# Reordering the pair loop of a chunk-selecting attention with a routed MoE behind it

## The chip, the cores and the metric

One core of one Trainium2 chip runs the whole program. The metric is the device time of one execution in microseconds; lower is better. The engines have these names in the profile: PE is TensorE (matmuls and transposes; PEld its weight loads), DVE is VectorE, ACT is ScalarE, POOL is GpSimd, and SP is the engine that issues most of the plain DMAs.

## The reference

```python
ub = np.sum(np.maximum(q * k_min, q * k_max), axis=-1)      # 24 chunks of 32 keys, per query
ub = np.where(causal, ub, -1e9)
top_chunks = np.argsort(ub, axis=-1)[..., -6:]
scores = scale * np.matmul(q, k.transpose(0, 1, 3, 2))
mask = sel & (pos[:, None] >= pos[None, :])                 # sel: the key's chunk is in top_chunks
scores = np.where(mask, scores, -1e9)
attn = softmax(scores)
x = (attn @ v), heads side by side                          # 3072 tokens of 512
expert_idx = np.argmax(x @ w_gate, axis=1)                  # top 1 of 8 experts
out[mask] = gate_w * (np.maximum(x[mask] @ w1[e], 0) @ w2[e])
```

There are 4 batches of 8 heads, 768 positions, head dimension 64. The expert layer has 512 inputs and 1024 hidden units. All inputs and outputs are float32.

## The kernel before

The attention works on pairs of heads of one batch: 16 pairs (`NP`), pair `i` being heads 2·hp and 2·hp+1 of batch b, with `b, hp = divmod(i, 4)`. The 128 partitions hold the two heads side by side. The loop over `i` is a schedule written out by hand: under `tc.manual_schedule` every engine executes its instructions in the order in which they stand in the program. Each pass mixes work of several pairs. For pair `i` it has the scores, the exponentials and the products with v; for `n = i + 1` the chunk selection; for `m = i + 2` the transposes of k and q; for pairs `i - 1` and `i - 2` the sums for the softmax, the gate's logits and the rows of x that go to the experts.

The steps, with the names that the prediction uses:

- `k_mm(hf)` transposes three 128-row tiles of k into a PSUM tile `pk`; `k_a` (ACT, L203) writes them as bf16 into KTE; `k_v` (DVE, L197 and L198) reduces them to each chunk's maximum and minimum; `kse` (DVE, L208 to L210) makes from these the operand KSD of the bounds.
- `q_mm(hf)` transposes q into `pq`; `q_v` (DVE, L223) copies it to `qT`; `q_a` takes the absolute value on ACT (`qA`, L228) and writes head 1's part of QSB (L231), and puts head 0's part (a POOL copy, L229) into the list `late`, which `flush(late)` issues.
- `ub` (L238) is four products of KSD with `qT` and four with `qA`: the upper bounds, chunk by query, in `pu`. `ub_a` (ACT, L245) copies them, `sel_mm` (L250) transposes them into `pt`, and `sel_v` (DVE) adds the causal bias `cbias` (L256), finds the eight largest of each row twelve times (L264) and marks in `nsel` what falls outside the six best (L267).
- `mask` (L274) transposes `nsel` into `pm`, and `mask_a` (ACT, L280) copies it into extra rows of QSB, so that the score product itself adds the mask.
- `scores(i, u)` (L298) makes one of seven units of scores (`units`: query block 0 has units 0 and 1, block 1 units 2 to 6; each 768 columns over two heads). `exps` is the ACT exponential (L314), with POOL's `affine_select` (L318) on diagonal tiles. `av(i, u)` (L331) is the product with v, added up in `po`; `add` (DVE, L339) adds up the exponentials for the row sums; `o_ev(i, qb)` copies `po` out (L344 on ACT, L346 on DVE).
- `ud` (L362 and L374, four column tiles of the array) makes the row sums and the gate's products of pair i-1; `ud_a` (L380), `lgp_mm` (L385), `lgp_v` (L391, L395), `x_mm` (`px`, L415) and `x_v` (L420) turn them into logits and rows. The logits are added on POOL by `sums` (L403, L406), which `flush(sums_)` issues.
- In the pairs with hp = 1 of batches 1 to 3 (called router pairs) also the routing of the batch before: `logits`, `rank_mm` (a PSUM tile `pr`, L467), `expo`, `rank_v`, `gates`. Its scatter of rows to DRAM (POOL, L493) is spread over that pair and the next by `spread`.

PSUM is shared out in three pools: `ps_m` has three buffers under one tag and holds `pk`, `pq`, `pu`, `pt`, `pm`, `pl` and `px` in turn; `ps_s` has two, for score units and `pr`; `ps_o` has one, for `po`.

PE's products come in three array shapes: the full array (scores except unit 6, and all float32 transposes), two column tiles of 64 (`av`, `ub`, the `nsel` transposes and score unit 6) and four column tiles of 32 (`ud`).

The weights of the experts come in 32 pieces by POOL's DMA queue (`load_w`, L157), spread over the pairs by `npiece`. `load` fetches k, q and v by SP's. `first_pair` builds constants and takes pair 0 up to its fourth score unit, in an order of its own. After the last pairs an expert table is computed on DVE (`table`), rows are gathered by POOL (`gather`, L593), transposed by DMA (`x_in`, L605), and each of 25 row tiles goes through `up` (L641) and `down` (L653), then out by a scatter (L661).

Of the kernel before, what the change touches and what calls it, by code (L numbers as in the profile page):

```python
# [24 lines left out]
def kernel(  # L25
# [33 lines left out]
    c0s = (0, 128, 192)  # L59
    NU = 7  # L60
# [23 lines left out]
    pm64 = const.tile([128, 1], FP32)  # L84

# [17 lines left out]
    def consts_first():  # L103
# [17 lines left out]
        nc.gpsimd.memset(cbias[:], 0.0)  # L121
        for t in range(3):
            nc.gpsimd.affine_select(out=cbias[:, t], in_=cbias[:, t], pattern=[[320, 2], [-CH, NCH]],
                                    compare_op=ALU.is_ge, fill=NEG, base=128 + c0s[t], channel_multiplier=1)
        nc.gpsimd.memset(nsel[:], 0.0)
# [10 lines left out]
        return colf  # L136
# [7 lines left out]
    def consts_last():  # L144
        nc.gpsimd.memset(dcol[:], 0.0)
        nc.gpsimd.memset(dcol[:, DC:DC + 1], 1.0)
        nc.gpsimd.memset(wgb[:], 0.0)

# [33 lines left out]
    def prep_steps(i):  # L182
# [70 lines left out]
        def sel_v():  # L253
            pt = s["pt"]
            ubm = work.tile([128, 3, 2, 2, NCH], FP32, tag="ubm")
# [85 lines left out]
    def o_ev(i, qb, act=False):  # L341
        ot = work.tile([128, 384], FP32, tag="ot", bufs=3, name="ot")
        if act:
            nc.scalar.activation(ot[:], st[i][f"po{qb}"][:], AF.Copy)  # L344
        else:
            nc.vector.tensor_copy(out=ot[:], in_=st[i][f"po{qb}"][:])  # L346
        st[i][f"ot{qb}"] = ot
# [326 lines left out]
    npiece = [1, 2, 2, 2, 2, 1, 1, 2, 2, 1, 1, 2, 2, 2, 4, 1]  # L674
    assert sum(npiece) == 4 * E - 4
# [6 lines left out]

    def first_pair():
# [4 lines left out]
        colf = consts_first()  # L688
# [34 lines left out]

        kt(0)
        for hf in range(2):
            nc.vector.tensor_copy(out=qsb[0:64, 1, ts(hf, 384)], in_=pq[64:128, hf, 0:384])
            nc.gpsimd.tensor_copy(out=qsb[0:64, 0, ts(hf, 384)], in_=s["qT"][0:64, hf])
        consts_last()
        consts_route(colf)
        prep[0]["ub"]()  # L730
        prep[0]["ub_a"]()
        kt(1)
        spin(8)
        prep[0]["sel_mm"]()
        spin(20)
        ubm = work.tile([128, 3, 2, 2, NCH], FP32, tag="ubm")
        top8 = work.tile([128, 3, 2, 2, 8], FP32, tag="top8")
        pm = ps_m.tile([64, S], BF16, tag="m")
        for _ in range(2):
            load_w(next(wnext))  # L740

        def select(hf):
            nc.vector.tensor_tensor(ubm[:, :, hf], s["pt"][:, :, hf, :, 0:NCH],
                                    cbias[:, :, hf].unsqueeze(2).to_broadcast([128, 3, 2, NCH]), ALU.add)
            for t in range(3):
                for hd in range(2):
                    nc.vector.max(out=top8[:, t, hf, hd], in_=ubm[:, t, hf, hd])
            nc.vector.tensor_tensor(nsel[:, :, hf, :, 0:NCH], ubm[:, :, hf],
                                    top8[:, :, hf, :, TOPK - 1:TOPK].to_broadcast([128, 3, 2, NCH]), ALU.is_lt)

        def mask_mm(hf):
            for t in range(3):
                nc.tensor.transpose(pm[:, ds(128 + 320 * hf + c0s[t], 128)],
                                    nsel[:, t, hf].rearrange("p a n -> p (a n)"), ident_b[:])

        def mask_in(hf):
            cols = ds(128 + 320 * hf, 320)
            nc.scalar.activation(qsb[64:64 + NCH, 0, cols], pm[0:NCH, cols], AF.Copy)
            nc.vector.tensor_copy(out=qsb[64:64 + NCH, 1, cols], in_=pm[32:32 + NCH, cols])

        select(0)
        mask_mm(0)
        mask_in(0)
        spin(8)
        scores(0, 0)
        exps(0, 0)
        select(1)
        scores(0, 1)
        exps(0, 1)
        mask_mm(1)  # L770
        mask_in(1)
        for _ in range(2):
            load_w(next(wnext))
        p1 = prep[1]
        for hf in range(2):
            p1["k_mm"](hf)
            p1["k_v"](hf)
            p1["k_a"](hf)
        p1["kse"]()
# [3 lines left out]
        p1["q_mm"](0)  # L783
        scores(0, 3)
        p1["q_mm"](1)
        av(0, 1)
        for hf in range(2):
            p1["q_v"](hf)
            p1["q_a"](hf, 0)
        load(2, "q")  # L790
        wg_v = moe_w_gate.rearrange("(c p) e -> p c e", p=128)
        nc.sync.dma_start(out=wgb[0:64, :, 0:E], in_=wg_v[0:64])
        nc.sync.dma_start(out=wgb[64:128, :, E:2 * E], in_=wg_v[64:128])
        exps(0, 2)
        exps(0, 3)
        o_ev(0, 0)
# [3 lines left out]
        for hf in range(2):  # L800
            p1["q_a"](hf, 1)

# [4 lines left out]
    with tc.manual_schedule(engines={PE, POOL, SP, DVE, ACT}):  # L807
        first_pair()
        early_table = table(True)
        for i in range(NP):  # L810
# [9 lines left out]
            for g in range(4):  # L820
                if (i, g) == (0, 0):
                    pass
                elif g == 0:
                    if i < NP - 1 and not (hp == 2 and b > 0):
                        pieces(i, 2 if router else 1)
                    if router:
                        logits()
                    for u in (2, 3):
                        scores(i, u)
                        exps(i, u)  # L830
                    run(rout, i - 2, "x_mm", 1)

                    xv_first = i < NP - 1 and (hp != 2 or b == 0)
                    if xv_first:
                        run(rout, i - 2, "x_v", 1)
                    if i < NP - 1:
                        add(i - 1, 5)
                    add(i - 1, 6)
                    if not xv_first:
                        run(rout, i - 2, "x_v", 1)  # L840
                    av(i, 0)
                    av(i, 1)
                    dve_ot = not router and i < NP - 2
                    if dve_ot or i == NP - 1:
                        o_ev(i, 0, not dve_ot)
                    add(i, 1)
                    run(prep, n, "ub")
                    run(prep, n, "ub_a")
                    if not dve_ot and i < NP - 1:
                        o_ev(i, 0, True)  # L850
                    if i < NP - 1:
                        load(n, "v")
                elif g == 1:
                    for u in (4, 5):
                        scores(i, u)
                        exps(i, u)
                    run(prep, n, "sel_mm")
                    if i > 0:
                        run(prep, m, "k_mm", 0)
                        run(prep, m, "k_a", 0)  # L860
                    if router:
                        rank_mm()
                    run(prep, n, "sel_v")
                    if router:
                        expo()
                        rank_v()
                        gates()
                    if i > 0:
                        run(prep, m, "k_v", 0)
                    av(i, 2)  # L870
                    av(i, 3)
                    add(i, 3)
                    flush(late)
                    if i < NP - 1:
                        pieces(i, 4)
                    scores(i, 6, True)
                    exps(i, 6)
# [165 lines left out]
```

The softmax here doesn't subtract the row's maximum and nothing guards it: scores larger than these inputs give would overflow.

## Time and profile before

| | |
|---|---|
| time, median of 3 runs | 357.44 us (356.74 to 357.91) |
| profiled execution | 357.17 us, of which the profile's span is 355.5 us |
| mean granted TensorE clock | 0.988 |
| L362 of pair 1 / of pair 14 starts at | 38.79 us / 218.25 us |
| intervals between L362 groups, pairs 2 to 14 | 13.38, 13.40, 13.50, 14.15, 14.22, 13.83, 13.50, 14.16, 13.97, 14.29, 13.51, 14.15, 13.40 us |
| first score unit of pair 0, its unit 4, pair 1's unit 2 | 14.29, 22.22, 31.27 us |
| first expert product | 236.43 us |

The intervals show the pace of the loop: the group L362 is issued once a pair, always at the same place of the order. Pairs 5, 9 and 13 are the router pairs. In rows of the timeline the first number is the start in us, the second the time until the last of the group ends, and in brackets stands idle time before it and what ended that. In rows of busy time by stage the columns are the stretch, its length, and PE, PEld, DVE, ACT and POOL busy (with counts), then the granted clock, the DMA engines' share and GB/s. A row of waits gives who waited for whom, the total in us, how often, and the longest.

### The profile page before, as it was taken

What the parts mean: (1) busy time and instruction counts of PE and PEld (TensorE: products, weight loads), DVE (VectorE), ACT (ScalarE), POOL (GpSimd) and SP (SyncE); (2) the same over time, 40 slices, a digit from 0 to 9 for tenths busy, and PEclk for the clock granted to TensorE, in tenths of its full rate; (3) what the DMA queues carried; (4) which work ended last, traced back from release to release, by engine and by line L of the source; (5) the groups of instructions that cost most, each with busy time, mean ns of one, the idle gap of its engine ahead of it and who ended that gap; (6) DMA issues with size and microseconds to landing.
All of it is one profiled execution on the core that took longest, in us unless ns stands there. A gap on an engine that the chain in (4) does not pass through costs nothing. (4 is left out here: it accounts for less than half of the span.)

```text
span 355.5 us, 7585 instructions
## 1 busy us (share of the span) xinstructions
PE 329.2 (93%) x2382; PEld 177.2 (50%) x2392; DVE 229.5 (65%) x776; ACT 230.4 (65%) x373; POOL 186.7 (53%) x300
## 2 busy tenths in 40 slices
PE   7889999999999999999999999977995899999992
PEld 7545656556555555555565555534441344444440
DVE  6688999999999999999999999941730000000000
ACT  2588788788796887886887977613323454544551
POOL 8515434536475437284355477583574556655323
PEclk9999999999999999999999999989998999999999
DMA  9998998899585897765979954969694999998962
GB/s 175 205 209 152 167 184 169 153 190 167 104 211 113 161 178 155 152 171 114 186 137 181 182 122 113 209 124 197 137 227 121 227 185 216 194 231 160 216 154 80
DMA packets 132071, 59.83 MB, mean 168 GB/s; under 512 B 122811, under 2 KB 122813, under 8 KB 132032
## 3 DMA queue, kind: packets, MB, share of 16 engines
q1 hardware_dynamic: 120640, 29.91, 43.5%
q0 software_dynamic: 11392, 29.42, 40.0%
q8 instruction: 21, 0.34, 0.4%
q14 instruction: 18, 0.15, 0.1%
HBM read 56.14 MB, written 10.51 MB: 188 GB/s over the span
## 5 line engine op out<-in xcount | busy, mean ns | idle before, releaser
L339 DVE TENSOR_TENSOR Pa<-Pa,Pr 128x768 f32<-128x768 f32 (+2 forms) x109 | 80.5, 742 | 4.3
L318 POOL TENSOR_SCALAR_AFFINE_SELECT Pr<-Pr 128x256 f32<-128x256 f32 x78 | 36.9, 492 | 77.9 <-ACT Pr L314 77.9
L314 ACT ACTIVATE Pr<-ps 128x768 f32<-128x768 f32 x79 | 62.6, 819 | 10.7 <-ACT KTE L203 4.3
L653 PE MATMUL py<-w_all,hT 128*128 x220 | 52.4, 379 | 3.0 <-issue 1.7
L298 PE MATMUL ps<-QSB,KTE 128*128 128x384 bf16 (+4 forms) x352 | 50.4, 283 | 1.5 <-ACT Pr L314 0.2
L661 POOL DMA_INDIRECT out_dram<-y,ti_all x28 | 28.0, 1001 | 37.2 <-ACT y L660 32.1
L298 PEld LDWEIGHTS <-KTE 128*128 128x128 bf16 (+1 forms) x352 | 26.5, 102 | 28.4 <-issue 22.0
L641 PE MATMUL ph<-w_all,KTE 128*128 x116 | 31.1, 413 | 6.3 <-ACT h__3986 L644 3.6
L653 PEld LDWEIGHTS <-hT 128*128 128x128 bf16 x224 | 21.8, 98 | 29.5 <-issue 1.8
L314 ACT ACTIVATE Pa<-ps 128x768 f32<-128x768 f32 x32 | 26.0, 812 | 14.0 <-PE ps L298 12.6
L660 ACT ACTIVATE y<-py,gt_all 128x512 f32<-128x512 f32 x27 | 18.6, 687 | 25.0 <-PE py L653 19.4
L203 ACT ACTIVATE KTE<-pk 64x384 bf16<-64x384 f32 x60 | 29.3, 488 | 7.1 <-DVE kmn L198 6.7
L493 POOL DMA_INDIRECT xs_dram<-xrow,sli x24 | 25.6, 1065 | 7.8 <-issue 5.7
L641 PE MATMUL ph<-w_all,QSB 128*128 x94 | 22.6, 379 | 1.6 <-DMA QSB<-xgqT 1.5
L641 PEld LDWEIGHTS <-KTE 128*128 128x128 bf16 x120 | 12.3, 104 | 23.0 <-issue 9.6
L280 ACT ACTIVATE QSB<-pm 24x640 bf16<-24x640 bf16 x30 | 20.8, 692 | 2.8 <-PE pm L274 2.1
L614 DVE TENSOR_TENSOR ti_all<-xgqA,inv_i 128x1 int32<-128x1 int32 x9 | 1.4, 160 | 30.7 <-DMA xgqA<-xs_dram,grow 26.1
L157 POOL DMA_DIRECT2D w_all<-in_moe_w_dram x32 | 21.1, 663 | 0.0
L197 DVE TENSOR_REDUCE kmx<-pk 128x12 f32<-128x384 f32 x32 | 17.6, 549 | 3.2 <-PE pk L192 3.0
L593 POOL DMA_INDIRECT xgqT<-xs_dram,grow x14 | 14.8, 1058 | 9.1 <-issue 6.2
L593 POOL DMA_INDIRECT xgqA<-xs_dram,grow x14 | 14.4, 1029 | 8.6 <-issue 4.7
L614 DVE TENSOR_TENSOR ti_all<-xgqT,inv_i 128x1 int32<-128x1 int32 x8 | 1.3, 159 | 25.7 <-DMA xgqT<-xs_dram,grow 20.9
(318 smaller groups left out, 635.9 us busy)
## 6 DMA issues: line engine op xcount, KB each, us to landing
w_all<-in_moe_w_dram POOLq DMA_DIRECT2D x32, 512.0 KB
out_dram<-y,ti_all POOLq DMA_INDIRECT x28
t__115<-in_k_dram SPq DMA_DIRECT2D x2, 192.0 KB
t__118<-in_q_dram SPq DMA_DIRECT2D x2, 192.0 KB
t__121<-in_v_dram SPq DMA_DIRECT2D x2, 192.0 KB
t__218<-in_k_dram SPq DMA_DIRECT2D x2, 192.0 KB
t__240<-in_q_dram SPq DMA_DIRECT2D x2, 192.0 KB
t__243<-in_v_dram SPq DMA_DIRECT2D x2, 192.0 KB
```

Source lines behind the costliest of these rows:

```text
L157: nc.gpsimd.dma_start(out=dst, in_=src.rearrange("(c p) f -> p c f" if n < 2 else "(p c) f -> p c f", p=128))
L203: nc.scalar.activation(kte[0:64, hd, ts(hf, 384)], pt[64 * hd:64 * hd + 64, :], AF.Copy, bias=0.0, scale=0.125)
L280: nc.scalar.activation(qsb[64:64 + NCH, hd, 128:S], s["pm"][32 * hd:32 * hd + NCH, 128:S], AF.Copy)
L298: nc.tensor.matmul(ps[ds(h * n, n), hd, ds(c0, w)], lhsT=kte[:, hd, ds(kb * 128 + h * n, n)], rhs=qsb[:, hd, ds(qb * 384 + 384 - w, w)], s ...
L314: nc.scalar.activation(P[:], ps[:, :, 0:384], AF.Exp)
L318: nc.gpsimd.affine_select(out=pd, in_=pd, pattern=[[0, 2], [1, 128]], compare_op=ALU.is_ge, fill=0.0, base=0, channel_multiplier=-1)
L339: nc.vector.tensor_tensor(acc[:, :, 384 - w:384], acc[:, :, 384 - w:384], P[:, :, ds(c0, w)], ALU.add)
L493: d = nc.gpsimd.indirect_dma_start(out=xs_dram[:], out_offset=bass.IndirectOffsetOnAxis(ap=sli[:, u:u + 1], axis=0), in_=bst[b][f"xrow{u % ...
L593: d = nc.gpsimd.indirect_dma_start(out=xg_bufs[j % XB].bitcast(I32), out_offset=None, in_=xs_dram[:], in_offset=bass.IndirectOffsetOnAxis( ...
L641: nc.tensor.matmul(ph[:, fh, :], lhsT=xT[:, c, :], rhs=w_all[:, ds(wo + (c * F + fh * 512), 512)], start=(c == 0), stop=(c == NDC - 1), sk ...
L653: nc.tensor.matmul(py[:], lhsT=hT[:, c, :], rhs=w_all[:, ds(wo + (W1W + c * DM), DM)], start=(c == 0), stop=(c == NFC - 1))
L661: d = nc.gpsimd.indirect_dma_start(out=out[:], out_offset=bass.IndirectOffsetOnAxis(ap=fs[j]["ti"], axis=0), in_=y[:], in_offset=None, bou ...
```

## The change

It rewrites the order of the pair loop and of `first_pair`.

- In the loop, selection of the next pair (`sel_mm`, `sel_v`) moves up beside units 2 and 3; `mask` goes between the transposes of k and `av` 2; `ud` stands between `av` 2 and `av` 3; `mask_a` follows `ud_a` on ACT; `av` 4, 5 and 6 stand together at the end, followed by `ub` and `ub_a` of pair i+2. `k_a` stands ahead of `k_v` in both halves. `flush(sums_)` moves to the end of each pair, `add(i, 5)` to the same pair's end.
- `o_ev` is on ACT by default, except for block 0 of pair 0.
- A one-element POOL copy `pace` out of `ubm` stands ahead of `flush(late)`, so that POOL's q copies follow the first step of `sel_v`.
- In `first_pair` the bounds of pair 0 come directly with queries on the partitions (`bounds`: five blocks of 128 queries, two products of 48 columns each), without `ub`, `ub_a` and `sel_mm`; constants of their own (`cb0`, `ns0`) stand in for `cbias` and `nsel`, which are built later. `consts_late` (routing constants, gate weights) moves to the end of pair 0.
- The four weight pieces inside `first_pair` go; `npiece` now covers all 32.

The diff, cut to its core:

```diff
-    def o_ev(i, qb, act=False):
+    def o_ev(i, qb, act=True):
...
-    npiece = [1, 2, 2, 2, 2, 1, 1, 2, 2, 1, 1, 2, 2, 2, 4, 1]
-    assert sum(npiece) == 4 * E - 4
+    npiece = [2, 3, 2, 2, 2, 2, 1, 2, 2, 2, 1, 2, 3, 2, 3, 1]
+    assert sum(npiece) == 4 * E
...
+        def bounds(js):
+            pt = ps_m.tile([128, len(js), 2, NCH], FP32, tag="m", name="pt0")
+            for n, j in enumerate(js):
+                for w_, nm in ((0, "qT"), (1, "qA")):
+                    nc.tensor.matmul(pt[:, n], lhsT=s[nm][:].rearrange("p a c -> p (a c)")[:, ds(128 * j + 128, 128)],
+                                     rhs=KSD[0][:, w_, :, 0:NCH], start=(nm == "qT"), stop=(nm == "qA"),
+                                     skip_group_check=True)
+            pts_.append(pt)
...
+        qsb_in(0)
         kt(0)
...
         consts_last()
-        consts_route(colf)
-        prep[0]["ub"]()
-        prep[0]["ub_a"]()
+        consts_bias()
+        bounds(halves[0])
+        select(0)
+        qsb_in(1)
+        spin(4)
+        bounds(halves[1])
         kt(1)
-        spin(8)
-        prep[0]["sel_mm"]()
-        spin(20)
...
-        for _ in range(2):
-            load_w(next(wnext))
...
+        p1["k_mm"](0)
+        p1["k_a"](0)
+        mask_mm(1)
...
+        p1["k_v"](0)
+        p1["k_mm"](1)
         load(2, "k")
         av(0, 0)
         scores(0, 2)
-        p1["q_mm"](0)
+        exps(0, 2)
+        p1["k_a"](1)
+        p1["k_v"](1)
+        p1["kse"]()
         scores(0, 3)
...
         for hf in range(2):
+            p1["q_mm"](hf)
             p1["q_v"](hf)
             p1["q_a"](hf, 0)
         load(2, "q")
-        exps(0, 2)
+        av(0, 1)
         exps(0, 3)
-        o_ev(0, 0)
+        o_ev(0, 0, False)
...
+            if i > 0:
+                if i < NP - 1 and not (hp == 2 and b > 0):
+                    pieces(i, 2 if router else 1)
+                if router:
+                    logits()
+                for u in (2, 3):
+                    scores(i, u)
+                    exps(i, u)
+                run(rout, i - 2, "x_mm", 1)
+                run(prep, n, "sel_mm")
+                add(i - 1, 6)
...
+                run(prep, n, "sel_v")
+                if n < NP:
+                    nc.gpsimd.tensor_copy(out=pace[:], in_=st[n]["ubm"][:, 0, 0, 0, 0:1])
+                    flush(late)
...
+                av(i, 0)
+                av(i, 1)
+                o_ev(i, 0)
...
+            for u in (4, 5):
+                scores(i, u)
+                if u == 5:
...
+                        if router:
+                            rank_mm()
+                            expo()
+                            rank_v()
+                            gates()
+                        run(prep, m, "k_mm", 0)
+                        run(prep, m, "k_a", 0)
+                        run(prep, n, "mask")
+                exps(i, u)
+            if i > 0:
+                add(i, 1)
+                run(prep, m, "k_v", 0)
+            av(i, 2)
+            run(rout, i - 1, "ud")
+            run(rout, i - 1, "ud_a")
+            if i > 0:
+                run(prep, n, "mask_a")
+            av(i, 3)
+            add(i, 3)
...
+            scores(i, 6, True)
+            exps(i, 6)
...
+            run(rout, i - 1, "lgp_mm")
+            run(rout, i - 1, "x_mm", 0)
...
+            run(rout, i - 1, "lgp_v")
+            run(rout, i - 1, "x_v", 0)
+            run(prep, m, "k_mm", 1)
+            run(prep, m, "k_a", 1)
+            if n < NP:
+                for u in (0, 1):
+                    scores(n, u)
+                    exps(n, u)
+            run(prep, m, "k_v", 1)
+            for hf in range(2):
+                run(prep, m, "q_mm", hf)
+                run(prep, m, "q_v", hf)
+                run(prep, m, "q_a", hf, 0)
+            for hf in range(2):
+                run(prep, m, "q_a", hf, 1)
...
+            run(prep, m, "kse")
...
+            av(i, 4)
+            av(i, 5)
+            av(i, 6)
...
+            o_ev(i, 1)
+            run(prep, m, "ub")
+            run(prep, m, "ub_a")
+            flush(sums_)
```

## The prediction

> **What bounds the kernel now.** I read the engine line of the page first, then busy time by stage, then waits inside the pair loop, then the timeline of one pair. About 200 of the 355.5 us are the sixteen head pairs, and the edits are nearly all there.
>
> ```profile
> PE 329.2 (93%) x2382; PEld 177.2 (50%) x2392; DVE 229.5 (65%) x776; ACT 230.4 (65%) x373; POOL 186.7 (53%) x300
> ```
>
> ```profile
> 65.57:79.07 13.50, 13.43 (x116) 7.65 (x113) 12.61 (x38) 11.20 (x19) 6.42 (x13) 1.00 0.87 170
> ```
>
> The second row is one plain pair, from its group L362 to the next one's: 13.50 us with PE busy 13.43, DVE 12.61, ACT 11.20. The page's average hides that two engines are nearly full here. The waits from 40 to 225 us:
>
> ```profile
> PEld px L415 <- ACT KTE L203: 3.9, 13, 0.4
> ...
> ACT KTE L203 <- DVE kmn L198: 5.2, 13, 0.5
> ...
> DVE lgt L395 <- POOL lg L406: 2.4, 6, 0.4
> ```
>
> DVE waits for almost nothing else: it has about 13.1 us of work a pair and 0.4 us of wait for POOL's sums. PE's own waits are small and come once a pair. In the pair at 65.57 I find, by comparing equal groups, about 0.27 us at score unit 5, 0.1 at `px` and under 0.1 twice more. So PE's floor is near 13.05 us, and a full relief of DVE can give at most 0.45 us a pair.
>
> [...] readers of one PSUM tile take turns in program order, whichever is first.
>
> ```profile
> 9.49 1.03 DVE L726 CAST QSB<-pq 64x384 bf16<-64x384 f32 x2 [0.56 <-ACT qT L716]
> ...
> 71.55 0.98 ACT L203 ACTIVATE KTE<-pk 64x384 bf16<-64x384 f32 x2 [0.39 <-DVE kmn L198]
> 72.59 0.31 PEld L415 LDWEIGHTS px<-ident_f,ot 128*128 128x128 f32 x3 [0.28 <-ACT KTE L203]
> ```
>
> In line 1 DVE waits for ACT's read of `pq`, in line 2 ACT for DVE's read of `pk`. Line 3 shows a second rule: the three `ps_m` buffers go round, and `px` may start only when the tile three allocations earlier (`pk` of half 1) has been read. [...] Here a group of three transposes takes 0.38 us before another full-array group (76.50 to 76.88) and 0.47 before a two-tile group (72.59 to 73.06), so some 0.1 to 0.16 us a change. [...] L406 takes 1.54 us for two beside the adds, 0.39 us for one away from them.
>
> **The change, part by part.**
>
> *Groups.* Before, a pair goes: full; `av` 0, 1 and `ub`; full; `av` 2, 3, unit 6, the four-tile `ud`, `pm`, `av` 4, 5; full; `av` 6. That is three full and three two-tile stretches with one four-tile group inside: eight changes. After: full; `av` 0, 1; full; `pm`, `av` 2, `ud`, `av` 3, unit 6; full; `av` 4, 5, 6, `ub`. Eight again, so nothing is saved on PE and the floor stays 13.05.
>
> *Outputs on ScalarE.* Two DVE copies of 0.55 us (0.47 each from start to start) become ACT copies of 0.50. DVE falls to 12.2, ACT rises from 11.2 to about 12.2. DVE then isn't the limit, and no longer waits for POOL's sums, which move to the pair's end. What is late next is ACT, and what it orders.
>
> *A plain pair after*, with t = 0 at unit 2, from these rows: 0.33 a score unit or three transposes (0.38 the first of a kind), 0.65 an `av` (0.70 the first), 0.1 to 0.16 a mode change, 1.18 `ub` with its change, exp 0.70 from start to start, KTE or Q copies 0.49. Unit 2, 3, `px`, `pt` to 1.44; `av` 0, 1 to 2.95; unit 4, 5, `pk` to 4.07; `pm`, `av` 2 to 5.13; `ud` to 6.23, its second half starting at 5.79. ACT: the new output copy waits for `av` 1 (3.1 to 3.6; exp 4 is queued behind it, price nothing because ACT had idled), exp 4 to 4.3, KTE to 5.3, exp 5 to 6.0. Then the first chain:
>
> ```profile
> 79.74 0.51 PE L374 MATMUL pu<-ot,wgb 128*32 128x192 f32 x8
> ...
> 80.38 0.49 ACT L380 ACTIVATE ud<-pu 128x384 f32<-128x384 f32 x1 [0.34 <-PE pu L374]
> 80.89 1.41 ACT L280 ACTIVATE QSB<-pm 24x640 bf16<-24x640 bf16 x2
> ...
> 82.31 0.49 PE L415 MATMUL px<-ident_f,ot 128*128 128x128 f32 x3
> ```
>
> Copy of `ud` 0.64 after its half begins, then both mask copies, 2.6 us in all before the `pm` buffer is free: 5.79 + 2.61 = 8.40. Today two `av` fill that span. After, PE has only `av` 3, unit 6 and `pl` in it, and is at `px` (three allocations after `pm` now) at 7.79. **Stall one: 0.61 us.** Then `pk` half 1 ends at 9.28. The change puts KTE ahead of the reduces on it, [...] the second chain is KTE 0.98 (9.28 to 10.26), two reduces 0.93, q copies 0.93, `kse` 0.56: KSD is ready at 12.72. PE reaches `ub` at 12.50. **Stall two: 0.25 us.** Unit 2 of the next pair comes at 12.78 + 1.18 = 13.96, against 13.45 before. ACT's last copies end at 14.69, 0.73 into the next pair, before `pt` needs them at 1.02; DVE's `nsel` at 3.85 is in time for `pm` at 4.07.
>
> *Router pair*, 14.15 before. `pr` is now the second score buffer after unit 4, so it waits for exp 4, behind the output copy: about 0.8 us. The logits stand ahead of the selection on DVE and `pl` waits a little for the reduces; `px` comes at about 9.6 instead of 8.4: 15.15. *The pair after it*: scatters (1.09 us each) go behind the q copies on POOL, whose next select is not due before 6; `x_v` behind the selection delays `pm` by some 0.35: 14.3, against 14.0 to 14.3.
>
> *POOL's other edits.* The one-element pace copy holds POOL's queue (q copies, and scatters) until the bounds exist near 2.2 us; q copies at 2 x 0.5 are beside top-8, as they already are at 78.28 today. Price nothing, 0.5 either way if selects slip. Weight pieces (0.66 us each on POOL) only move; by pair 13 as many have gone as before.
>
> *Sum over the thirteen intervals* from the L362 group at 38.79 to that at 218.25, 179.5 us: 7 x 13.96 + 3 x 15.15 + 3 x 14.3 = 186.1, **+6.6**. Each stall is good to 0.25 us, so -1 to +10.
>
> *Start.* Direct bounds drop `ub`, its copy and three transposes, but add ten fp32 products with full-array weights, in no row. Bounds: 0.14 us a weight load as L415's, or 0.4 a product as L238's; I take 0.3, so 3 us, part of it under the first selection. First scores then stand near 14.2 against 14.29. Four weight pieces leave the first 28 us, so the k load awaited at 26.43 (0.96 us) is early. Against it, KTE, reduces, q copies, |q| and exp 3 now stand in one chain (KTE to 19.2, q copies to 21.6, exp 3 to 22.9), and unit 4 comes near 22.5 to 23 instead of 22.22; `consts_late` (1.1 us of DVE) stands in pair 0 after `kse`, hidden by `av` 4 to 6. I take **+1**, bounds -3 and +2.
>
> *End.*
>
> ```profile
> 227.28 1.09 POOL L593 DMA_INDIRECT xgqT<-xs_dram,grow  x1 [2.21 <-issue]
> ...
> 233.02 2.67 SPq L605 DMA_TRANSPOSE KTE<-xgqT  x2
> ...
> 236.43 5.30 PE L641 MATMUL ph<-w_all,KTE 128*128 x15 [2.03 <-DMA KTE<-xgqT]
> ```
>
> The first gathers wait for the table, then 5.7 us pass to the transposes, and PE waits 2 us. After, the table is complete earlier in pair 14 and three pieces instead of four stand ahead of them, so that wait may go: **-2**, bounds -3 and 0.
>
> Sum 6.6 + 1 - 2 = +5.6 on the profiled execution's 357.17 (span 355.5 and 1.67 around it), 362.8; the median 357.44 is 0.27 above, so **363.0**.
>
> **Rivals.** *Faster: DVE was the bound and nothing takes its place.* For it: DVE's lack of waits, and ACT's 0.39 us wait for `kmn` that disappears. Against it: the two chains. It decides from the point where the mask copies end before 7.79 and KSD before 12.50. With 13.05, 13.6 and 13.2 the loop is 171.8, -7.7; start -1, end -2: 347. With half of each stall it is 354. Chance 0.20. *No change*, 357 within 1 us: one stall stays and start and end pay for it; 0.07. *Slower by the stalls*, 358.5 to 369, my forecast: 0.70. *Slower by DMA*: weights moved behind pair 0 delay the k, q, v loads. For it: the DMA share of 0.87 in the pair above. Against: the waits show no loop stall on a load. It costs if a load lands over 5 us later, some 0.5 us a pair, 364; 0.03. *That the change isn't what it says*: the three and three groups exist already, by my count, so this part can't bring the gain its name suggests.
>
> A difference of 0.3% (1.1 us) is about what can be told from none here. The range 351 to 369 leaves out the fast half of the first rival.
>
> **What would show it.** Right: `px` L415 waiting for ACT's mask copies L280 by about 0.6 us once a pair; `ub` L238 waiting for KSD by 0.2 to 0.3; `pr` waiting for exp; a plain pair near 14.0, DVE with idle time. Wrong: plain pairs at or under 13.3, `px` without a wait, or the first unit 4 before 21 us.

## The result, and the profile after

The changed kernel takes 373.34 us (median of four runs, 368.63 to 374.75), the kernel before 357.09 in the same job. The ratio, 1.0377 with a 95% interval of 1.0275 to 1.048, compares only the two faster of the four runs, because the other two, the profiled one among them, lie over 1.5% above the fastest. In a later job, with seven runs of the kernel before, it is 1.0466 (1.0396 to 1.0536). The change is slower, as forecast, but by 16 us instead of 5.6, and outside the range. The profiled execution takes 374.40 us, span 372.6. Times differ from chip to chip (the kernel before has medians from 351.9 to 357.4), so ratios below are always to the kernel before on the same chip. Line numbers of the changed kernel are ten higher in the loop: L362 is now L372.

The engine row of the page, after:

```profile
PE 331.1 (89%) x2372; PEld 178.3 (48%) x2372; DVE 226.2 (61%) x750; ACT 241.8 (65%) x396; POOL 188.0 (50%) x317
```

PE has the same work as before (331.1 us busy for 329.2) and a smaller share of the span, 89% for 93%: the time went into waiting. The work did move from DVE to ACT. One plain pair by stage, from the start of one `ub` to the next (columns as before):

```profile
65.30:79.48 14.18, 13.45 (x113) 7.80 (x113) 12.38 (x36) 12.16 (x23) 6.13 (x14) 1.00 0.89 156
```

14.18 us where the kernel before needs 13.50; DVE and ACT are now equally full, neither has more than 12.4 of the 14.18. The waits of PE between 40 and 235 us say who holds it up:

```profile
PE pu L248 <- DVE KSD L220: 5.6, 10, 0.6
PE pk L202 <- ACT QSB L290: 2.8, 13, 0.5
PE pu L384 <- DMA wgb<-in_moe_w_gate_dram: 2.6, 1, 2.6
```

The second comes in each of the thirteen pairs and the first in ten of them; they are the forecast's two stalls. The third comes once and was not forecast. In rows of the timeline just ahead of the stage row above, the chain can be followed from engine to engine:

```profile
59.22 1.40 ACT L290 ACTIVATE QSB<-pm 24x640 bf16<-24x640 bf16 x2
60.66 0.31 PEld L202 LDWEIGHTS pk<-ident_f,t__738 128*128 128x128 f32 x3 [0.40 <-ACT QSB L290]
61.35 0.97 ACT L213 ACTIVATE KTE<-pk 64x384 bf16<-64x384 f32 x2
62.35 0.56 DVE L207 TENSOR_REDUCE kmx<-pk 128x12 f32<-128x384 f32 x1 [0.67 <-PE pq L229]
...
64.76 0.40 DVE L220 TENSOR_TENSOR KSD<-kt,bm 128x96 f32<-128x96 f32 x1
65.27 0.23 PEld L248 LDWEIGHTS pu<-qT,KSD 128*64 128x64 f32 x4 [0.77 <-ACT qA L238]
```

The mask copies end at 60.62, and only then, at 60.66, does PE load for `pk`. KTE reads `pk` from 61.35 to 62.32; DVE had been idle for 0.67 us and starts its reduce as ACT leaves the tile. (The row names `pq` as the releaser, but the start coincides with the end of KTE.) KSD is ready at 65.16 and `ub` follows. The row for the weight load of `ub` names ACT's `qA` and PE's own wait names KSD. `qA` was ready at 64.82, 0.34 us ahead of KSD, so it is KSD that holds `ub` here.

Where the 17.2 us between the two profiled executions lie, by points that can be compared (the last column is the forecast, +5.6 in all):

| stretch | before | after | difference | forecast |
|---|---|---|---|---|
| to unit 2 of pair 1 (in the kernel before plus 1.2 us for `ub`, which the changed one has done by then) | 32.5 | 35.54 | +3.05 | +1 |
| 13 intervals of the L362/L372 group | 179.46 | 191.51 | +12.05 | +6.6 |
| last of these to the first expert product, less the 1.46 us by which the group stands earlier in its pair (6.3 us behind the first row's point before, 4.84 after) | 18.18 | 22.02 | +2.4 | -2 |
| from there to the end, and outside the span | 120.7 | 120.5 | -0.3 | 0 |

The 1.46 us of the third row is measured in pair 1. In pair 14, where unit 2 starts at 211.38 us before and 226.46 after, the same measure gives only 0.24, so some 1.2 us may belong to the end instead of the loop.

### The profile page after: what moved, and what is told of

Its sections match the earlier page's. It is cut to its first block, busy times and chain, and to the rows that moved or that the text cites. A ratio compares the mean times of both kernels' runs of the same rounds, so it can differ in the third digit from the quotient of the medians.

```text
span 372.6 us, 7610 instructions
## 1 busy us (share of the span) xinstructions
PE 331.1 (89%) x2372; PEld 178.3 (48%) x2372; DVE 226.2 (61%) x750; ACT 241.8 (65%) x396; POOL 188.0 (50%) x317
## 5 line engine op out<-in xcount | busy, mean ns | idle before, releaser
L349 DVE TENSOR_TENSOR Pa<-Pa,Pr 128x768 f32<-128x768 f32 (+2 forms) x109 | 82.4, 757 | 5.4 <-POOL Pa L328 0.5
L328 POOL TENSOR_SCALAR_AFFINE_SELECT Pr<-Pr 128x256 f32<-128x256 f32 x78 | 32.8, 439 | 75.2 <-ACT Pr L324 75.1
L324 ACT ACTIVATE Pr<-ps 128x768 f32<-128x768 f32 x79 | 63.7, 809 | 1.8 <-DVE Pa L349 1.1
L651 PE MATMUL ph<-w_all,KTE 128*128 x120 | 29.8, 395 | 7.7 <-DMA KTE<-xgqT 4.7
L354 ACT ACTIVATE ot<-po 128x384 f32<-128x384 f32 x31 | 15.2, 491 | 16.6 <-PE po L341 16.3
L416 POOL TENSOR_TENSOR lg<-lg,lgt 128x96 f32<-128x96 f32 x24 | 16.9, 705 | 7.0 <-DVE lgt L405 6.0
```

Source lines behind the costliest of these rows:

```text
L324: nc.scalar.activation(P[:], ps[:, :, 0:384], AF.Exp)
L328: nc.gpsimd.affine_select(out=pd, in_=pd, pattern=[[0, 2], [1, 128]], compare_op=ALU.is_ge, fill=0.0, base=0, channel_multiplier=-1)
L349: nc.vector.tensor_tensor(acc[:, :, 384 - w:384], acc[:, :, 384 - w:384], P[:, :, ds(c0, w)], ALU.add)
L651: nc.tensor.matmul(ph[:, fh, :], lhsT=xT[:, c, :], rhs=w_all[:, ds(wo + (c * F + fh * 512), 512)], start=(c == 0), stop=(c == NDC - 1), sk ...
```

## The experiments

**Gate weights.** The DMA that brings `wgb` has moved from `first_pair` to the end of pair 0. The timeline of the changed kernel, a DMA row of SP's queue and the group that needs it:

```profile
33.43 5.44 SPq L825 DMA_DIRECT2D wgb<-in_moe_w_gate_dram  x1
...
43.88 0.53 PE L384 MATMUL pu<-ot,wgb 128*32 128x192 f32 x8 [2.64 <-DMA wgb<-in_moe_w_gate_dram]
```

The edit puts the load back where it was, with nothing else changed:

```diff
         load(2, "q")
+        wg_v = moe_w_gate.rearrange("(c p) e -> p c e", p=128)
+        nc.sync.dma_start(out=wgb[0:64, :, 0:E], in_=wg_v[0:64])
+        nc.sync.dma_start(out=wgb[64:128, :, E:2 * E], in_=wg_v[64:128])
         av(0, 1)
...
     def consts_late():
         consts_route(colf_[0])
-        wg_v = ...
```

> The changed kernel with the two loads of the gate's weights put back into pair 0's opening, ahead of av 1. Theory A (late gate weights hold ud of pair 1): the wait of L384 for wgb (2.6 us on PE, 3.3 on its weight loads) goes, the interval from pair 1's ud to pair 2's falls from 17.0 to 14.2 us, and the time by 2.8 us from the changed kernel's. Rival (the pair is late for another reason, the weights only come last): the interval stays above 16 us and the time within 1 us.

Measured: 363.22 us (362.88 to 363.53), ratio 1.0314 (1.0263 to 1.0365). The interval from pair 1 to pair 2 is 14.17 us instead of 17.01, and the row has lost its wait:

```profile
40.98 0.51 PE L384 MATMUL pu<-ot,wgb 128*32 128x192 f32 x8
```

So the late load costs 2.84 us. In this run the 13 intervals add to 186.79 us, +7.3 against the kernel before: without this wait, and without the late signals that the control below shows (this run has none), the loop is near the forecast's +6.6.

**The opening.** In the changed kernel fewer filler products keep PE busy in `first_pair` (`spin`), and the granted clock of its first profile shows a stretch at half speed from 11.5 to 18.4 us. Two rows of the stage table from 10 to 20 us, first of the changed kernel's first profile:

```profile
10.00:20.00 10.00, 9.52 (x56) 5.65 (x55) 4.46 (x19) 5.57 (x12) 2.47 (x10) 0.66 0.51 94
```

then of the same kernel in a later run (the control below):

```profile
10.00:20.00 10.00, 7.88 (x63) 5.10 (x62) 6.41 (x26) 6.28 (x13) 2.82 (x12) 1.00 0.61 119
```

In the first PE is 9.52 us busy with fewer instructions at a granted clock of 0.66; in the second the clock is 1.00. This edit adds filler products to the changed kernel:

```diff
         qsb_in(1)
-        spin(4)
+        spin(10)
         bounds(halves[1])
...
-        spin(4)
+        spin(12)
         mask_mm(0)
+        spin(8)
```

> The changed kernel with idle products on PE raised around pair 0's bounds and first mask: 10 and 12 instead of 4 and 4, and 8 more after the mask's transposes. Theory (the half clock from about 11.4 to 18.3 us comes from an opening with few products in flight): no half-speed stretch before 20 us, the first scores group 0.5 us shorter, pair 0's unit 4 near 23 instead of 24.3 us, time 1 to 2 us less. Rival (the clock drops independently of what runs): the half-speed stretch stays or appears elsewhere, and the time is unchanged or up to 1 us more for the extra products.

Measured: 364.47 us (363.91 to 370.12), ratio 1.0344 (1.0283 to 1.0405), beside 1.0314 for the kernel above on the same chip, which has its gate weights early; here they are still late, and the interval from pair 1 to pair 2 is 15.44 us, 1.27 longer. The stretch before 20 us is gone, but one of 3.41 us stands at 22.5 us, behind a wait of 2.27 us of PE for `qA`; the L372 group of pair 1 comes at 40.20 against 40.31 in the kernel above. Up to that point nothing is gained. More filler was tried again at the end, on the mended kernel, with the same result. Over all profiles, seven of ten executions with the new opening have a half-speed stretch that begins before 30 us, and none of four with the old one. That points at the new opening rather than at chance alone; what in it sets the stretch off was not found.

**Reduces ahead of KTE.** If ACT's read of `pk` ahead of DVE's delays KSD, the old order should help.

```diff
             run(prep, m, "k_mm", 1)
+            run(prep, m, "k_v", 1)
             run(prep, m, "k_a", 1)
...
-            run(prep, m, "k_v", 1)
```

> The changed kernel with the reduces of k's second half ahead of the ACT copies of it in the loop (k_v before k_a), as in the kernel before. Theory A [...]: DVE no longer waits 0.67 us there, KSD is ready 1.1 us sooner, the 0.56 us wait of ub for KSD goes, a plain pair falls from 14.18 to 13.6 us, the time by 6 to 8 us. Rival B (ACT is as late itself): ub then waits for qA instead, since copies and the two exponentials move back by 0.8 us; a plain pair stays above 13.9, the time within 3 us of the changed kernel's.

Measured: 371.21 us (369.3 to 376.87), ratio 1.0523 (1.0454 to 1.0591), a plain pair 14.48 us. The waits of PE from 60 to 230 us now begin with

```profile
PE pu L248 <- ACT qA L238: 9.9, 12, 1.0
```

The wait for KSD is gone and one of up to 1.0 us for `qA` has its place: KTE now waits for the reduces (it starts at 76.28 us, as they end at 76.19, after ACT has idled 1.25 us), and the exps and q copies behind it on ACT are later with it. With either order the engine that reads `pk` second holds `ub`, DVE in the changed kernel and ACT here, and the old order is the dearer one. So swapping the reads is no cure.

**Outputs on ACT without the new order.** The kernel before with every output copy on ACT (block 0 of pair 0 excepted):

```diff
-                    if dve_ot or i == NP - 1:
-                        o_ev(i, 0, not dve_ot)
+                        o_ev(i, 0, True)
...
-                    o_ev(i, 1, i >= NP - 2)
+                    o_ev(i, 1, True)
```

> The kernel before with both output copies on ACT in every pair but block 0 of pair 0, at the same places of the order. Theory A (DVE was full but PE's own work sets the pair): at most the 0.4 us of PE waits can go; a plain pair 13.2 to 13.5 us, 352 to 358 us. Rival (DVE was the bound): a plain pair falls to 13.05 us and the time to 350 us. Third (ACT becomes late, exp 3 holds unit 5 for longer): a plain pair 13.8 us or more, 362 us.

Measured: 392.2 us (388.43 to 395.41), ratio 1.1101 (1.1019 to 1.1183), a plain pair near 17.0 us. Slower was expected by one theory, for another reason than the one at work. First a row of PE's waits between 60 and 200 us:

```profile
PE po L331 <- issue: 16.2, 8, 2.0
```

and from the timeline, in an ACT row and a PE row:

```profile
153.67 0.49 ACT L344 ACTIVATE ot<-po 128x384 f32<-128x384 f32 x1
154.06 0.81 ACT L314 ACTIVATE Pa<-ps 128x768 f32<-128x768 f32 x1
...
154.26 1.55 PE L331 MATMUL po<-Pa,t__1871 128*64 128x384 f32 x4 [2.03 <-issue]
```

`av` 0 starts as the output copy of block 1 ends, though the row names only "issue". The copy stands behind four q copies on ACT, and there is one `po` buffer. Thirteen such gaps of 2.03 us lie between 49 and 254 us of this trace; ten of them run into a 3.41 us stretch at half clock, which is part of the loss (the granted clock of the pair from 144.63 to 161.69 us is 0.90), and three do not.

**Only block 0 on ACT.** The same with block 1 left on DVE, so that only the first of the two edits above is made.

> Kernel before with only the copies of output block 0 on ScalarE (block 1 stays on VectorE). Theory A (the earlier experiment with both on ScalarE lost its time at block 1, which stands behind four q copies while the one po buffer is held): no wait of av 0 for po; ubT is 0.5 us later on ScalarE, pt waits 0.2 to 0.5 us, plain pair 13.6 to 13.9, ratio 1.005 to 1.02. Theory B (VectorE bounds the kernel before): plain pair 13.1 to 13.3, ratio 0.98 to 0.99. Theory C (block 0 on ScalarE holds po as well): plain pair over 14.5.

Measured: 355.06 us against 352.52, ratio 1.0072 (1.0047 to 1.0096); plain pairs 13.77 to 13.90 us, no wait for `po`. Nearly all the loss of the experiment above is therefore block 1's. What remains is one row of the timeline, PE's weight loads:

```profile
78.05 0.31 PEld L250 LDWEIGHTS pt<-ident_f,ubT 128*128 128x128 f32 x3 [0.62 <-ACT ubT L245]
```

The same place in the kernel before shows 0.24 us. And DVE, relieved of a copy, did not make the pair shorter. In the new order `av` 4 and 5, `ub` and `pt` stand in addition between the transposes of q and the next `av` 0, which leaves the block 1 copy more time. That this is what makes the outputs on ACT bearable there is argued from the order; no run tries it alone.

**Control.** The changed kernel once more, beside the next three on one chip.

> The changed kernel unchanged, beside the experiments that follow on the same chip. If the late gate weights cost 2.8 us, as the experiment that loads them earlier says, this stands 2.5 to 3.5 us over that kernel's ratio to the kernel before: ratio near 1.04. If the two agree (1.031), the late load was hidden after all. The pair interval 1 to 2 should be near 17.0 us, plain pairs 14.17.

Measured: 373.21 us (371.89 to 375.58) against 357.11, ratio 1.0466 (1.0396 to 1.0536). Plain pairs 14.17, pair 1 to 2 17.09. In two pairs, those with the second half of the scatters (pair 6 and its like in the next batch), ACT waits far longer for the `ud` group than it takes. Three rows of this run's timeline:

```profile
113.69 0.51 PE L384 MATMUL pu<-ot,wgb 128*32 128x192 f32 x8
...
115.74 0.49 ACT L390 ACTIVATE ud<-pu 128x384 f32<-128x384 f32 x1 [1.85 <-PE ps L308]
...
116.28 0.55 PE L395 MATMUL pl<-ident_f,ud 128*128 128x128 f32 x3 [0.96 <-ACT ud L390]
```

and the same copy in the kernel with the early gate weights:

```profile
113.20 0.49 ACT L390 ACTIVATE ud<-pu 128x384 f32<-128x384 f32 x1 [0.46 <-PE pu L384]
```

The trace's semaphore record has the signal of that group's end 1.78 us after its last product starts, where 0.37 us is usual, while PE goes on with `av` 3 and unit 6. These pairs take 15.58 and 15.59 us instead of 14.17; in the first profile of the changed kernel 14.96 and 15.07, with the signal after 1.15 and 1.27 us. Why the signal is late was not found, nor why the profiles of the first three experiments on the changed kernel, from another chip, show no such wait.

**Mask copies first.** The forecast's first chain says that the copy of `ud`, then both mask copies, then everything behind follow PE's `ud` group. ACT idles 0.44 us before the copy of `ud`, with `pm` ready. The edit uses that:

```diff
+            if i > 0:
+                run(prep, n, "mask_a")
             av(i, 2)
             run(rout, i - 1, "ud")
             run(rout, i - 1, "ud_a")
-            if i > 0:
-                run(prep, n, "mask_a")
...
-            run(rout, i - 1, "lgp_mm")
             run(rout, i - 1, "x_mm", 0)
+            run(rout, i - 1, "lgp_mm")
```

> Changed kernel, with ScalarE's two mask copies issued ahead of the copy of ud instead of behind it, and the transposes px issued ahead of pl. Nothing is added or left out. Theory A (the chain ud group, copy of ud, mask copies, exp of unit 6, KTE, reduces, q copies, KSD, ub sets the pair): the masks fill ScalarE's 0.44 us idle time before the copy of ud, so everything behind them is 0.4 us earlier; the wait of ub for KSD falls from 0.56 to 0.1 to 0.2, a plain pair is 13.7 to 13.8 instead of 14.17, 13 intervals give 5 us less. Theory B (ScalarE's amount of work, 12.4 us, with VectorE's, sets the pair, in whatever order): plain pair stays at 14.1 to 14.2. Theory C (VectorE is already late by itself through the reads of pk and pq): wait for KSD stays 0.4 or more, pair 14.0 to 14.2.

Measured: 366.99 us (365.75 to 368.69), ratio 1.0285 (1.022 to 1.0351), 6.2 us under the control. Plain pairs take 13.99 us, by stage

```profile
68.56:82.55 13.99, 13.55 (x114) 7.82 (x112) 12.45 (x35) 12.14 (x22) 6.27 (x13) 1.00 0.93 163
```

and of PE's waits from 60 to 230 us the first is

```profile
PE pu L248 <- DVE KSD L220: 3.0, 8, 0.4
```

The row for `pk` is gone. DVE and ACT have the same work as in the changed kernel (12.45 and 12.14 us for 12.38 and 12.16), so it is the order, not the amount, that cost this time. The edit also puts `px` ahead of `pl`; the two moves were not tried apart. But 0.2 us of a plain pair came back, not 0.4 to 0.5, because `ub` still waits 0.37 us for KSD. Router pairs gain 0.17, the pairs after them some 0.45, and the two late signals no longer show, since the copy of `ud` now comes later anyway.

**Outputs back on DVE.** This undoes one part of the change alone.

```diff
-                o_ev(i, 0)
+                o_ev(i, 0, router or i >= NP - 2)
...
-            o_ev(i, 1)
+            o_ev(i, 1, i >= NP - 2)
```

> Changed kernel, with the output copies given back to VectorE where the kernel before had them (block 0 outside router pairs, block 1 everywhere but the last two pairs). ScalarE loses 1.0 us a pair, VectorE gains 1.1. Theory A (the chain from the ud group to ub sets the pair; output copy 0 stands before that chain on ScalarE and output copy 1 after it): nothing is gained; VectorE's 0.9 us of idle time in a pair is used up, plain pair 14.1 to 14.6. Theory B (outputs on ScalarE made it the bound): plain pair 13.6 to 13.8, some 6 us less in all.

Measured: 373.56 us (371.34 to 374.88), ratio 1.0433 (1.0363 to 1.0502), the same as the control's within the intervals. One plain pair by stage:

```profile
71.39:85.60 14.21, 13.49 (x115) 7.83 (x113) 12.96 (x38) 11.23 (x20) 6.27 (x13) 1.00 0.91 157
```

ACT has 0.9 us less and the pair is 14.21 us. Where the outputs are copied makes no difference in the new order: neither copy sets the pair.

**Gathers and sums.** At the end, the first gathers stand behind pair 14's sums on POOL in the new order. Rows of the changed kernel's first profile:

```profile
240.11 0.17 DVE L572 SCALAR_TENSOR_TENSOR grow<-ej,loc 128x11 int32<-128x11 f32 x1
...
240.86 1.59 POOL L416 TENSOR_TENSOR lg<-lg,lgt 128x96 f32<-128x96 f32 x2 [2.35 <-DVE lgt L405]
242.60 1.37 POOL L603 DMA_INDIRECT xgqT<-xs_dram,grow  x1 [0.15 <-issue]
...
253.91 0.59 PE L651 MATMUL ph<-w_all,KTE 128*128 x1 [4.65 <-DMA KTE<-xgqT]
```

The edit issues these sums behind the first two gathers:

```diff
                 for j in range(2):
                     gather(j)
                     x_in(j)
+                flush(sums_)
...
-            flush(sums_)
+            if i != NP - 2:
+                flush(sums_)
```

> Changed kernel, with pair 14's sums on GpSimd issued behind the first two gathers of pair 15 instead of ahead of them. Nothing else changes. Theory A (the gathers queue behind the sums, which wait for VectorE's lgt): gathers start about 2.3 us sooner, near 1 us after the last select of the pair; the wait of the first up group for its transposes falls from 4.65 to about 2.4 us, and the whole is 2 to 2.5 us shorter. Theory B (the gathers wait for the table of rows or for the DMA queue): no change within 1 us.

Measured: 374.8 us (374.63 to 376.87), ratio 1.0508 (1.0439 to 1.0576): no gain in the whole. The timeline of this run:

```profile
241.51 0.17 DVE L572 SCALAR_TENSOR_TENSOR grow<-ej,loc 128x11 int32<-128x11 f32 x1
242.48 1.10 POOL L603 DMA_INDIRECT xgqT<-xs_dram,grow  x1 [2.57 <-issue]
```

The gather starts 0.8 us after the table's last instruction ends, as in the kernel before (226.31 and 0.17, then 227.28). So the sums cost 1.5 us and the table sets the rest. From the last L372 group to the first expert product it is 17.2 us here, 18.7 in the control. In the whole they don't show: this profiled execution has ten us of half clock in its opening, the control none, and its L372 group of pair 1 comes at 42.50 instead of 38.23.

**The mended kernel.** Mask copies first, gate weights early, gathers ahead of sums, together.

> Changed kernel with three edits together: mask copies ahead of the copy of ud and px ahead of pl (as tried), gate weights loaded after pair 2's q as the kernel before did (as tried), gathers of pair 15 ahead of pair 14's sums (as tried). If the costs add, 6.2 us (masks), 2.8 us (gate weights) and 0 to 1.5 us (sums) come off the changed kernel: ratio to the kernel before 1.014 to 1.022 instead of 1.047. The rest, 5 to 8 us, is then the KSD wait of 0.4 us a pair that stays with ub at the pair's end, the router pairs, and the opening. If the edits overlap (one wait behind another), ratio 1.022 to 1.028.

Measured: 360.96 us (356.88 to 361.27) against 352.52, ratio 1.0214 (1.0144 to 1.0284), from 1.0466: the gains of the first two add (6.2 and 2.8 us are 9.0 us, 2.5 points of the kernel before's 357.1, and 2.5 points are measured). It is still slower than the kernel before. The 13 intervals are 184.35 us, against 179.46 before: 4.9 us of the loss is the loop, with `ub` still waiting some 0.38 us for KSD in ten of the pairs.

**The mended kernel with more filler products**, the edit as above.

> The mended changed kernel, with the spin products of the opening at 10 and 12 plus 8 in place of 4 and 4. Theory A (the half-speed stretches of TensorE's clock in the opening come from too little TensorE work there): no half-speed stretch before 20 us, granted clock higher by about 0.01, time 1 to 3 us under the mended kernel without them. Theory B (the stretches come by chance or from elsewhere): the same time within 1 us, or up to 1 us more for the added products.

Measured: 359.35 us (357.03 to 362.03), ratio 1.0188 (1.0107 to 1.027): not told apart from the mended kernel. Two of its runs take 357.03 at granted clocks of 0.998 and 0.999 and two about 361.9 at 0.982 and 0.992; of the mended kernel one takes 356.88 at 0.998, three about 361 at 0.977 to 0.984. Runs at nearly full clock exist with either number of products.

**One q copy later.** From the other side: can the kernel before be made faster where its PE waits about 0.27 us at the group of score units 4 and 5, for an exp that stands behind four q copies?

```diff
-                        run(prep, m, "q_a", hf)
+                        run(prep, m, "q_a", hf, *((0, 1) if hf == 0 else (0,)))
...
                         exps(i, u)
+                    run(prep, n, "q_a", 1, 1)
                     run(rout, i - 2, "x_mm", 1)
```

> Kernel before with one of the four q copies of a pair (QSB of the second half, head 1) issued on ScalarE behind the exps of units 2 and 3 of the next pair instead of ahead of them. Theory A (score unit 4 waits 0.27 us for the exp of unit 2, which stands behind four q copies): exps 0.5 us earlier, the wait goes, plain pair 13.2 to 13.3, 14 pairs, 2.5 to 4 us less, ratio 0.989 to 0.993. Theory B (VectorE's 13.1 us a pair is the bound, or ubT, which now stands behind the same copies, holds pt back): plain pair 13.4 to 13.5, ratio 0.998 to 1.002.

Measured: 352.79 us against 352.52, ratio 1.0 (0.9967 to 1.0034). A weight load of PE in this run:

```profile
76.68 0.31 PEld L250 LDWEIGHTS pt<-ident_f,ubT 128*128 128x128 f32 x3 [0.47 <-ACT ubT L245]
```

The group no longer waits (0.82 us instead of 1.05; in the trace of the kernel before the wait stands at unit 5, as the prediction has it, for the exp of unit 3), and `pt` waits 0.47 instead of 0.24: what was won went to the next instruction behind the moved copy. None of the versions tried beats the kernel before.

## Why the prediction was right or wrong

The direction and the mechanism of the loop were right, the size of the whole was not. Of the 11.6 us between the forecast's +5.6 and the +17.2 of the two profiles, 5.45 lie in the loop, 4.4 at the end and 2.05 in the opening, less 0.3 behind these, by the table above. The loop's part is the step that failed outright: `consts_late`, called hidden, cost 2.84 us, and most of the rest is the late signals. Point by point:

- **No saving on PE, eight changes of array shape.** Right as far as it shows: taking the two weight-load waits (0.40 and 0.77 us) from 14.18 leaves 13.01, the forecast's floor being 13.05.
- **Stall one, 0.61 us at `px`.** The chain was right: with the masks moved out of it the row is gone. Who waits was wrong, `pk` and not `px`, and the size is 0.40 by the weight loads, 0.16 by PE's products. The step that failed is "three allocations after `pm`": in the pair above the copy of `ud` ends at 59.19 us and the mask copies at 60.62, and `px` starts at 60.02, so it did not have to wait for the mask's buffer.
- **Stall two, 0.25 us at `ub`.** Right in place and cause, too small: 0.56 on PE, 0.77 by the weight loads. The term that was mis-sized is `kse`, which takes 0.94 us from 64.22 to 65.16 instead of 0.56. In that time POOL is at its selects and at the sums of the logits, and these sums are what the change has moved to the pair's end; in the kernel before, in the pair that the forecast read, POOL was idle there. The changed kernel's profile has both cases. In the three router pairs POOL issues a scatter at that place, the same instructions take 0.56 us, and `ub` waits only 0.18 us. Rows of the pair above, then of pair 13:

```profile
64.31 0.41 DVE L219 TENSOR_TENSOR kt<-kmx,kmn 128x24 f32<-128x24 f32 x1
64.65 1.62 POOL L416 TENSOR_TENSOR lg<-lg,lgt 128x96 f32<-128x96 f32 x2
...
224.62 0.17 DVE L219 TENSOR_TENSOR kt<-kmx,kmn 128x24 f32<-128x24 f32 x1
224.82 0.26 DVE L220 TENSOR_TENSOR KSD<-kt,bm 128x96 f32<-128x96 f32 x1
225.23 0.76 PE L248 MATMUL pu<-qT,KSD 128*64 128x320 f32 x4 [0.17 <-ACT qA L238]
```

  In the reduce experiment POOL is idle beside `kse` in the plain pairs, and it takes 0.56 us there too. So about 0.38 of the 0.56 us comes with the neighbour on POOL. The forecast reckoned with such a neighbour for POOL's sums and not for `kse`. No edit moved POOL's selects or sums away from `kse` in the loop, so what that would gain is not shown.
- **Sum of the loop, +6.6.** With the gate weights early it is +7.3 (plain pairs 14.17 for 13.96, router pairs 15.24 for 15.15, the pairs after 13.83 for 14.3). That the sum fits so well is partly luck: the plain pairs cost some 1.5 us more than forecast and the three intervals after a router pair some 1.4 less; in these `ub` does not wait for KSD. The router pairs' own stall is as forecast, `pr` waiting for exp 4, 0.57 us instead of about 0.8. In the profile of the change it is +12.05: 2.84 for the gate weights, and some 1.9 for the late signals of pairs 6 and 10.
- **`consts_late` "hidden by `av` 4 to 6".** This step failed. It counted the DVE work that moves and forgot the two DMAs in the same function; they now stand behind pair 3's k and q on SP's queue, where their issue ended at 39.52 us, and the `ud` group of pair 0, ready for them at 41.24, started at 43.88. The cost is 2.84 us.
- **Opening, +1.** Right where the clock is full: in the control unit 2 of pair 1 comes at 33.40, +0.9. In the first profile it is +3.05; the other 2.15 us go with the half-speed stretch, which the forecast had no term for. The ten products of `bounds` cost 0.22 us each, not 0.3.
- **End, -2.** The reason given failed: "the table is complete earlier in pair 14" is not so, since its last instruction starts 8.2 us after that pair's L372 group where it was 8.1; three pieces ahead of the gather instead of four don't matter to that. The forecast also put nothing down for pair 14's sums, which now stand ahead of the first gather and cost 1.5 us. In the profile of the change the stretch is +2.4: 1.5 of it are the sums, and the transposes, issued at 248.08, let PE start only 5.8 us later (3.2 us in the run with the gathers ahead). In the five other profiled runs that leave the end as the change has it, the stretch is between 0.05 and 1.4 us shorter than before by the same measure, and between 0.2 shorter and 0.8 longer if it is counted from unit 2 of pair 14. So whether the end gains anything is open, the rest of the +2.4 belongs to that one execution, and what made its transposes late was not found.
- **The rival "DVE was the bound"** finds no support: a copy taken from DVE in the old order lengthened the pair, and two given back to it in the new order left the pair as it was.

What stays open: what sets off the half-speed stretches in the opening (more filler products did not prevent them), how much of a plain pair POOL's selects and sums beside `kse` cost, why the `ud` signal is late in two pairs and the transposes were in one execution, and how much of the remaining loss of the mended kernel, ratio 1.0214, lies outside the loop.

## What to carry to other kernels

Cost a moved function by everything it issues: here a loss of 2.8 us lay in two small DMAs inside a function that was moved for its DVE work. The chain through three engines was shortened by filling the head engine's idle time with what must be done anyway (mask copies before the copy of `ud`: a plain pair of 13.99 us for 14.17), not by lightening an engine that does not set the pace: giving two copies from ACT back to DVE moved nothing (14.21 us). Ask of what is moved whether it will stand beside another engine's work: `kse` took 0.94 us beside POOL's selects and sums, 0.56 us without them. When a consumer is placed at the end of a pair, count how much other work lies between it and its producer, since that is all the lateness it can bear.

## What the runs showed of the hardware

- TensorE's granted clock fell to half for whole stretches: 3.41 us from 237.7 and again from 271.8 us in the kernel before, 6.83 us from 11.5 and 3.41 us from 253.9 us in the change. On one chip the new opening had none in the control (1.00 from 10 to 40 us) and ten us of half speed in the run with the gathers ahead of the sums. With all outputs on ACT in the old order, ten of thirteen gaps of 2.03 us, one a pair, ran into a stretch of 3.41 us: the four products of `av` 0 took 1.55 us at 154.26, and 0.87 at 188.88, where the clock held. So a stretch can come with a gap of 2.03 us, though not each time. What sets it off was not shown.
- A wait row can name the wrong engine: the weight load of `ub` at 65.27 is put down to `qA`, ready since 64.82, while KSD came at 65.16.
- Three small DVE instructions (`kse`) took 0.94 us beside POOL's selects and sums (64.22 to 65.16 us in the change), and 0.56 us beside a scatter (224.53 to 225.08) or with POOL idle (77.04 to 77.60 in the reduce experiment).
- The signal of a finished PE group came 1.78 us after the start of its last product in two pairs of the control and 1.15 and 1.27 us in the same pairs of the change's profile, 0.37 us in others, while PE went on working.
